# Two VectorE instructions change places at the end of each output tile

## The chip, the cores and the metric

The kernel runs on one core of a Trainium2 chip (trn2). The metric is the device time of one execution in microseconds (us), as the median of several runs. One further execution was taken with the hardware profiler; all profile lines come from it.

## The reference

Two stages follow each other, for B = 4 batches of N = 12,480 tokens with C = 128 channels, and 49 agents per batch.

```python
def sm(a, b):
    s = scale * (a @ b.transpose(0, 2, 1))
    e = np.exp(s - s.max(-1, keepdims=True))
    return e / (e.sum(-1, keepdims=True) + 1e-09)
agent_v = sm(agents, k) @ v          # 49 x 128 for each batch
x = sm(q, agents) @ agent_v          # 49,920 tokens x 128
r = np.maximum(x @ w_in, 0.0)        # 2,048 hidden channels
out = (r * r) @ w_out                # 49,920 x 128
```

The kernel folds `agent_v @ w_in` into one weight `W` of 49 rows for each batch, so that the hidden channels come straight from the 49 probabilities of a token.

## The kernel before

**Precision.** The large products are made with pairs: a value is rounded to the matmul's format (`hi`, here `gh`), the remainder is a second value (`lo`, here `gl`), and TensorE adds three products: hi by hi, hi by lo, lo by hi.

**The main loop.** The 49,920 tokens fall into 104 output tiles of `TT` = 480 tokens. A tile has 8 steps (`NJ`), and each step handles 256 of the 2,048 hidden channels, 832 steps in all. Step `i` has these parts:

- `mm1(i)`, TensorE (L364): six matmuls give the hidden values `h`, two banks of PSUM; there are two such buffers.
- `relu(i)`, ScalarE (L370): reads `h` and writes half of a buffer `rg` for two steps, which are called a pair.
- After the odd step of a pair: `square`, ScalarE (L373), in place on the whole pair, 1,920 values per partition; `high`, VectorE (L377), rounds it to `gh`; `low`, VectorE (L381), writes the remainder `gl = rg - gh`. `rg`, `gh` and `gl` have three buffers each.
- `mm2(i - 5)`, TensorE (L392): twelve matmuls of the step that lies `LAG` = 5 back, eight that read `gh` and then four that read `gl`. They add into the tile's two output banks, because the 128 contraction rows are worked in two halves at the same time, one bank for each half.

**The tile end.** After the eighth `mm2` of a tile, `store` puts the two banks together: ScalarE copies the first bank to `ob` (L397), VectorE adds the second bank (L398), and a DMA on SyncE's queue writes `ob` out (L399).

**Who wants the banks next.** There are two pairs of output banks, `pair0` and `pair1`; the tiles take them in turn. While one collects a tile, the other serves the side work of later tokens and batches: q scores and k scores (L167), transposes of the q probabilities (L338), the sums over v (L226) and the weight `W` (L277). The first side work of a tile stands on TensorE behind two further steps after the tile end, and it writes the banks that `store` has just read. Side work on the other engines includes `v_lo` (L218), `v_sum` (L242), `q_shift` (L299, L304) and `k_pmax` (L177) on VectorE, some casts on ScalarE (L214, L342), and subtractions and products on GpSimd (POOL). It is densest in three stretches of the run, in which a next batch's k and v are worked off.

**The order.** Every part is put on a list with a time, `at(t, f, ...)`, counted in steps; the list is sorted by time, and each engine gets its instructions in that order. The times are an order only: at run time each engine goes through its queue and waits where an input is missing. The set `ends` holds the steps at which a tile's last `mm2` stands (i - 5 = 7, 15, ...); each is an even step, so a pair's square, `high` and `low` come from the odd step just ahead of it. At the ends no side work is planned on ScalarE and VectorE.

Of the kernel before, what the change touches and what calls it, by code (L numbers as in the profile page):

```python
# [25 lines left out]
def agent_attention_relu2_kernel(ctx: ExitStack, tc: tile.TileContext, qT, kT, v, agT, w_in, w_out, outT):  # L26
# [379 lines left out]
    def at(t, f, *args):  # L406
        steps.append((t, len(steps), f, args))
# [5 lines left out]
    ends = {i for i in range(NG + LAG) if i >= LAG and (i - LAG) % NJ == NJ - 1}  # L413
# [172 lines left out]
    for i in range(NG + LAG):  # L586
        if i < NG:
            at(i, mm1, i)
            at(i + .1, relu, i)
            if i % 2:  # L590
                at(i + .55, square, i // 2)
                at(i + .6, high, i // 2)
                at(i + .65, low, i // 2)
        if i >= LAG:
            at(i + .2, mm2, i - LAG)
            if i in ends:
                at(i + .2, store, (i - LAG) // NJ)
# [28 lines left out]
```

## Time and profile before

| | us |
|---|---|
| median of 3 runs | 2093.01 |
| lowest and highest | 2086.31, 2101.51 |
| the profiled execution's own time | 2085.59 |
| its span, from the first to the last instruction | 2083.8 |
| TensorE (PE) busy | 2006.3 |
| weight loads (PEld) busy, beside the matmuls | 1844.0 |
| VectorE (DVE) busy | 1766.4 |
| ScalarE (ACT) busy | 1729.2 |
| GpSimd (POOL) busy | 301.2 |

The mean granted clock of TensorE is 0.984 of full speed. The DMA queues move 62 GB/s on average. In the profile's rows a name such as `ob<-ob,pair` gives the tile written and the tiles read; L398 is line 398 of the kernel. An arrow in brackets says how long the engine idled before an instruction and who ended that idle time.

### The profile page before, as it was taken

To read this page: it belongs to the slowest core of one execution; us is meant where nothing else is said; L and a number is where in the kernel's file an instruction comes from. 1 tells how busy PE (TensorE), PEld (TensorE's weight loads), DVE (VectorE), ACT (ScalarE), POOL (GpSimd) and SP (SyncE) were. 2 spreads that over 40 slices of the span, in tenths; PEclk is the share of its full clock that TensorE was granted. 3 is DMA by queue.
4 is the path that set the end of the run, shared out by engine and by line. 5 is a ranking of instruction groups with operands and counts; after the bars stand their busy time and mean duration, and the time that the engine had idled before them with its cause. 6 is when DMAs were issued, how large, how long until landed. Compare 5 with 4: busy or idle time off the path is not lost.

```text
span 2083.8 us, 45903 instructions
## 1 busy us (share of the span) xinstructions
PE 2006.3 (96%) x20130; PEld 1844.0 (88%) x20130; DVE 1766.4 (85%) x1513; ACT 1729.2 (83%) x1818; POOL 301.2 (14%) x199
## 2 busy tenths in 40 slices
PE   9899999999999999999999999999999999999999
PEld 8699988898899988988978988888887999999998
DVE  7688889899878889989887888987997888888888
ACT  2587888898878888988878788888888888888887
POOL 0100012321000102321100001232210111111010
PEclk9999999999999999999999999999999999999999
DMA  9422122121122122122112212222211111111110
GB/s 288 105 77 80 43 72 71 51 73 51 42 82 80 46 68 61 46 77 62 37 55 68 80 51 65 60 61 64 61 32 44 32 49 32 49 32 48 33 40 20
DMA packets 52849, 129.56 MB, mean 62 GB/s; under 512 B 5760, under 2 KB 21248, under 8 KB 52648
## 3 DMA queue, kind: packets, MB, share of 16 engines
q1 hardware_dynamic: 52648, 126.62, 21.3%
q8 instruction: 158, 2.59, 0.5%
q14 instruction: 43, 0.35, 0.1%
HBM read 81.47 MB, written 25.56 MB: 51 GB/s over the span
## 4 chain that ended last, share of the span: by engine, by line
PE 52%; ACT 19%; DVE 15%; issue 12%; POOL 1%; DMA 1%; SPq 0%; DVEq 0%; POOLq 0%; ACTq 0%
PE pair L392 23%; PE h L364 15%; ACT rg L373 10%; PE pair L167 8%; DVE gh L377 7%; ACT rg L370 7%; DVE gl L381 3%; PE pair L338 2%; DVE ob L398 2%; PE pair L226 1%; DVE vs L218 1%; POOL e L323 1%; PE h L167 1%; DMA vt<-v 1%; PE pair L277 1%
## 5 line engine op out<-in xcount | busy, mean ns | idle before, releaser
L370 ACT ACTIVATE rg<-h 128x960 f32<-128x960 f32 x832 | 804.2, 972 | 279.0 <-PE h L364 277.4
L381 DVE TENSOR_TENSOR gl<-rg,gh 128x1920 fp32r<-128x1920 f32 x416 | 921.2, 2214 | 30.2 <-DVE gh L377 1.8
L373 ACT ACTIVATE rg<-rg 128x1920 f32<-128x1920 f32 x416 | 756.1, 1817 | 6.1
L377 DVE CAST gh<-rg 128x1920 fp32r<-128x1920 f32 x416 | 509.7, 1225 | 230.1 <-ACT rg L373 223.8
L392 PE MATMUL pair<-gh,wo_hi 64*128 64x480 f32 x3328 | 676.9, 380 | 3.2 <-DVE acc L240 2.5
L392 PE MATMUL pair<-gh,wo_lo 64*128 64x480 f32 x3328 | 677.9, 381 | 0.0
L364 PE MATMUL h<-p_b,w_hi 49*128 49x480 f32 x1664 | 650.8, 391 | 0.0
L364 PE MATMUL h<-p_a,w_hi 49*128 49x480 f32 x1664 | 649.4, 392 | 0.3
L392 PE MATMUL pair<-gl,wo_hi 64*128 64x480 f32 x3328 | 520.5, 378 | 0.3 <-DVE gl L381 0.3
L392 PEld LDWEIGHTS pair<-gh,wo_lo 64*128 64x128 f32 x3328 | 358.8, 188 | 22.5
L392 PEld LDWEIGHTS pair<-gh,wo_hi 64*128 64x128 f32 x3328 | 355.8, 187 | 25.7 <-DVE acc L240 3.3
L392 PEld LDWEIGHTS pair<-gl,wo_hi 64*128 64x128 f32 x3328 | 351.2, 186 | 20.2 <-DVE gl L381 0.7
L364 PEld LDWEIGHTS h<-p_a,w_hi 49*128 49x128 f32 x1664 | 311.4, 187 | 16.8 <-issue 6.4
L364 PEld LDWEIGHTS h<-p_b,w_hi 49*128 49x128 f32 x1664 | 311.6, 187 | 11.1
L364 PE MATMUL h<-p_a,w_lo 49*128 49x480 f32 x832 | 316.5, 380 | 0.0
L364 PE MATMUL h<-p_b,w_lo 49*128 49x480 f32 x832 | 316.4, 380 | 0.0
L323 POOL TENSOR_TENSOR e<-e,sm 120x392 f32<-120x392 f32 x52 | 55.4, 1065 | 1278.8 <-DVE sm L320 800.4
L364 PEld LDWEIGHTS h<-p_a,w_lo 49*128 49x128 f32 x832 | 158.1, 190 | 5.6
L364 PEld LDWEIGHTS h<-p_b,w_lo 49*128 49x128 f32 x832 | 158.1, 190 | 1.5
L206 POOL TENSOR_TENSOR pe<-sk,pe 120x392 fp32r<-120x392 f32 x39 | 77.1, 1976 | 304.4 <-ACT pe L203 257.7
L330 POOL TENSOR_TENSOR pp<-e,pp 120x392 fp32r<-120x392 f32 x52 | 101.9, 1959 | 91.2 <-ACT pp L327 91.0
L167 PEld LDWEIGHTS pair<-ag_sb,qt 64*120 64x120 f32 x1600 | 88.4, 182 | 29.3 <-DVE ob L398 29.3
(93 smaller groups left out, 1341.5 us busy)
## 6 DMA issues: line engine op xcount, KB each, us to landing
vt<-v SPq DMA_DIRECT2D x104, 243.8 KB
kt<-kT SPq DMA_DIRECT2D x52, 480.0 KB
qt<-qT SPq DMA_DIRECT2D x52, 480.0 KB
outT<-ob SPq DMA_DIRECT2D x104, 240.0 KB
p_b<-p_a SPq DMA_DIRECT2D x104, 183.8 KB
raw<-w_in SPq DMA_DIRECT2D x4, 512.0 KB
raw<-w_out SPq DMA_DIRECT2D x4, 512.0 KB
ag_sb<-agT SPq DMA_DIRECT2D x1, 196.0 KB
```

The costliest lines, as they stand in the source:

```text
L167: nc.tensor.matmul(ps[:CH, u, c * A:(c + 1) * A], x[rg[u], h, c, :], ag_sb[rg[u], b, h, :], start=h == 0, stop=h == 1)
L206: eng.tensor_tensor(out=pes[n][:, :, A:], in0=piece(n), in1=pes[n][:, :, :A].bitcast(F32), op=ALU.subtract)
L323: eng.tensor_tensor(out=es[s], in0=es[s], in1=sms.pop(s).to_broadcast([CH, G, A]), op=ALU.mult)
L330: eng.tensor_tensor(out=pps[s][:, :, L:], in0=es.pop(s), in1=pps[s][:, :, :A].bitcast(F32), op=ALU.subtract)
L338: nc.tensor.matmul(pss["t", s][u][:, c, :], pp[rc[u], c, :], ident_r[rc[u], rc[u]], start=True, stop=True)
L364: nc.tensor.matmul(h[:, u, :TT], w[ra[u], j, :], PT[s][u ^ lo][ra[u], cs, :], start=x == 0, stop=x == 2)
L370: nc.scalar.activation(rgs[p][:, x], hs.pop(i)[:, :, :TT], AF.Relu)
L373: nc.scalar.activation(rgs[p], rgs[p], AF.Square)
L377: nc.vector.tensor_copy(ghs[p], rgs[p])
L381: nc.vector.tensor_tensor(out=gls[p], in0=rgs.pop(p), in1=ghs[p].bitcast(F32), op=ALU.subtract)
L392: nc.tensor.matmul(outs[t][u][:, :TT], w[rg[u], 2 * j + e, :], g[rg[u], e, :], start=j == 0 and x == 0, stop=j == NJ - 1 and x == 5)
L398: nc.vector.tensor_tensor(ob, ob, o[1][:, :TT], op=ALU.add)
```

## The change

`low` of the pair that ends just ahead of a tile end gets the time i + 1.25 instead of i + 0.65. The tile end's `store` stands at i + 1.2 in the same count, so `low` falls behind it. All other pairs stay as they were.

```diff
             if i % 2:
                 at(i + .55, square, i // 2)
                 at(i + .6, high, i // 2)
-                at(i + .65, low, i // 2)
+                at(i + (1.25 if i + 1 in ends else .65), low, i // 2)
         if i >= LAG:
             at(i + .2, mm2, i - LAG)
             if i in ends:
                 at(i + .2, store, (i - LAG) // NJ)
```

The order changes on VectorE alone; TensorE, ScalarE, GpSimd and SyncE keep every instruction in its place. VectorE's queue around tile 39 (counted from 0), in one of the stretches with work for the next batch, before:

```order
L377 CAST gh<-rg 128x1920
L381 TENSOR_TENSOR gl<-rg,gh 128x1920
L377 CAST gh<-rg 128x1920
L381 TENSOR_TENSOR gl<-rg,gh 128x1920
L398 TENSOR_TENSOR ob<-ob,pair_105 128x480
L218 TENSOR_TENSOR vs_82<-vt,vs_82 120x4x128
L377 CAST gh<-rg 128x1920
```

And of the change at the same place:

```order
L377 CAST gh<-rg 128x1920
L381 TENSOR_TENSOR gl<-rg,gh 128x1920
L377 CAST gh<-rg 128x1920
L398 TENSOR_TENSOR ob<-ob,pair_105 128x480
L381 TENSOR_TENSOR gl<-rg,gh 128x1920
L218 TENSOR_TENSOR vs_82<-vt,vs_82 120x4x128
L377 CAST gh<-rg 128x1920
```

The add (L398) stands between the rounding and the subtraction of the same pair; what follows stays. VectorE's queue around tile 87, in the later part of the run, where no work for a next batch is left, before:

```order
L320 RECIPROCAL sm<-sm 120x8
L377 CAST gh<-rg 128x1920
L381 TENSOR_TENSOR gl<-rg,gh 128x1920
L377 CAST gh<-rg 128x1920
L381 TENSOR_TENSOR gl<-rg,gh 128x1920
L398 TENSOR_TENSOR ob<-ob,pair_105 128x480
L377 CAST gh<-rg 128x1920
```

And of the change:

```order
L320 RECIPROCAL sm<-sm 120x8
L377 CAST gh<-rg 128x1920
L381 TENSOR_TENSOR gl<-rg,gh 128x1920
L377 CAST gh<-rg 128x1920
L398 TENSOR_TENSOR ob<-ob,pair_105 128x480
L381 TENSOR_TENSOR gl<-rg,gh 128x1920
L377 CAST gh<-rg 128x1920
```

Here too the two instructions have changed places and the next pair's rounding follows directly.

## The prediction

> **What bounds the kernel now.** I read first how busy each engine is, then who waits for whom, then two tile ends instruction by instruction, and last the granted clock by stretches. The page's first rows:
>
> ```profile
> span 2083.8 us, 45903 instructions
> PE 2006.3 (96%) x20130; PEld 1844.0 (88%) x20130; DVE 1766.4 (85%) x1513; ACT 1729.2 (83%) x1818; POOL 301.2 (14%) x199
> ```
>
> TensorE (PE) sets the time: it stands still for 2083.8 - 2006.3 = 77.5 us in all. VectorE (DVE) and ScalarE (ACT) have 317 us and 355 us to spare. The waits say what each engine stands for (total us, times, longest). ScalarE, VectorE, TensorE and its weight loads:
>
> ```profile
> ACT rg L370 <- PE h L364: 277.4, 210, 4.0
> ```
>
> ```profile
> DVE gh L377 <- ACT rg L373: 223.8, 208, 2.7
> ```
>
> ```profile
> PE pair L338 <- DVE ob L398: 44.3, 50, 2.9
> PE pair L167 <- DVE ob L398: 11.3, 15, 1.4
> ```
>
> ```profile
> PEld pair L167 <- DVE ob L398: 29.3, 49, 1.8
> ```
>
> ScalarE waits 210 times for TensorE's `h`, VectorE 208 times for ScalarE's square: both catch up with TensorE again and again. TensorE's own large wait is for `ob`, the add that frees the output banks: 44.3 us in front of the transposes (L338) and 11.3 us in front of the q scores (L167), 55.6 us together. The 29.3 us on the weight loads of L167 are not added: weight loads run ahead of the matmuls, and 44.3 + 29.3 + 11.3 = 84.9 us would be more than the 77.5 us that TensorE idles.
>
> **Why the add is late: two tile ends.** Tile 39, in a stretch with work for the next batch. Of VectorE, ScalarE and TensorE, each with start and length in us:
>
> ```profile
> 879.54 1.93 DVE L377 CAST gh<-rg 128x1920 fp32r<-128x1920 f32 x1 [0.91 <-ACT rg L373]
> 881.58 2.73 DVE L381 TENSOR_TENSOR gl<-rg,gh 128x1920 fp32r<-128x1920 f32 x1
> 884.23 0.64 DVE L398 TENSOR_TENSOR ob<-ob,pair 128x480 f32<-128x480 f32 x1
> ```
>
> ScalarE's copy, and the transposes on TensorE:
>
> ```profile
> 880.24 0.58 ACT L397 COPY ob<-pair 128x480 f32<-128x480 f32 x1
> ```
>
> ```profile
> 885.02 0.97 PE L338 MATMUL pair<-ident_r,pp 64*113 64x64 f32 x16 [1.75 <-DVE ob L398]
> ```
>
> And tile 87, without such work:
>
> ```profile
> 1807.98 1.62 DVE L377 CAST gh<-rg 128x1920 fp32r<-128x1920 f32 x1 [0.28 <-ACT rg L373]
> 1809.70 2.16 DVE L381 TENSOR_TENSOR gl<-rg,gh 128x1920 fp32r<-128x1920 f32 x1
> 1811.78 0.65 DVE L398 TENSOR_TENSOR ob<-ob,pair 128x480 f32<-128x480 f32 x1
> 1812.34 1.15 DVE L377 CAST gh<-rg 128x1920 fp32r<-128x1920 f32 x1
> ```
>
> ```profile
> 1808.70 0.55 ACT L397 COPY ob<-pair 128x480 f32<-128x480 f32 x1
> ```
>
> ```profile
> 1812.57 0.98 PE L338 MATMUL pair<-ident_r,pp 64*113 64x64 f32 x16 [0.75 <-DVE ob L398]
> ...
> 1814.10 0.41 PE L392 MATMUL pair<-gh,wo_hi 64*128 64x480 f32 x2
> 1814.32 0.41 PE L392 MATMUL pair<-gh,wo_lo 64*128 64x480 f32 x2
> ```
>
> In both, ScalarE's copy, which the add needs, is done (880.82 and 1809.25) before VectorE ends `gh` (881.47 and 1809.60). The add waits for nothing but its place in the row: `gl` stands in front of it, until 884.23 and 1811.78. TensorE was ready at 885.02 - 1.75 = 883.27 and at 1812.57 - 0.75 = 1811.82.
>
> **The change part by part.** Nothing is added or removed; at each tile end but the last the add and the subtraction change places.
>
> *The wait for the add.* The add starts where `gl` started: 881.58 instead of 884.23 (2.65 us earlier) and 1809.70 instead of 1811.78 (2.08 us). It ends at 882.22 and 1810.35, before TensorE comes at 883.27 and 1811.82, so both waits go. The mean wait is 44.3 / 50 = 0.89 us and 11.3 / 15 = 0.75 us; only two are longer than the 2.1 us:
>
> ```profile
> 292.65 1.70 PE L338 MATMUL pair<-ident_r,pp 64*113 64x64 f32 x15 [2.86 <-DVE ob L398]
> ```
>
> ```profile
> 373.58 0.65 PE L338 MATMUL pair<-ident_r,pp 64*113 64x64 f32 x9 [2.50 <-DVE ob L398]
> ```
>
> They leave 0.8 us and 0.4 us. With as much again for tile ends at which VectorE comes later than now, I count 53 of the 55.6 us.
>
> *The new wait in front of the add.* VectorE must now stand until ScalarE's copy is done, with `gl` queued behind. That cannot gain anything; at the two tile ends it costs nothing, since the copy was done 0.65 us and 0.35 us before the end of `gh`. Where the copy ends together with `gh` it is some tenths of VectorE's spare time, which is 317 us. Term: 0; the other end is the slow rival below.
>
> *The subtraction comes later,* by the add's step in the row: 1812.34 - 1811.78 = 0.56 us. Its reader is the last third of a `mm2` behind the transposes. In tile 87 TensorE takes 1814.10 - 1812.57 = 1.53 us from the start of the transposes over `mm1` to that `mm2`, whose four groups of `gh` matmuls follow each other by 1814.32 - 1814.10 = 0.22 us, 0.88 us in all. Starting the transposes at 1811.82 it wants `gl` at 1814.23. It ends at 1809.70 + 0.56 + 2.16 = 1812.42, 1.8 us in time. In tile 39, with the same steps from 883.27, it is wanted at 885.68 and ends at 881.58 + 0.56 + 2.73 = 884.87, 0.8 us in time. So `gl` is what comes late next; its weight loads wait for it once today:
>
> ```profile
> PEld pair L392 <- DVE gl L381: 0.7, 1, 0.7
> ```
>
> *The store* is issued 2 us earlier on SyncE's queue, its order there unchanged; nobody waits for it. Term: 0.
>
> *The clock.* Stretches of the run: PE, PEld, DVE, ACT, POOL busy us (instructions), then granted clock, DMA share, GB/s:
>
> ```profile
> 95.00:260.00 165.00, 163.49 (x1774) 152.51 (x1771) 133.02 (x108) 134.31 (x137) 11.48 (x8) 1.00 0.22 64
> 260.00:540.00 280.00, 265.75 (x2640) 247.52 (x2642) 251.77 (x213) 244.60 (x267) 63.76 (x40) 0.98 0.23 63
> 540.00:740.00 200.00, 196.26 (x2057) 178.43 (x2056) 161.09 (x136) 161.27 (x170) 14.23 (x10) 0.99 0.22 64
> 740.00:1060.00 320.00, 305.97 (x2990) 284.18 (x2988) 280.35 (x238) 276.55 (x298) 69.33 (x42) 0.97 0.21 58
> 1060.00:1260.00 200.00, 196.12 (x2068) 176.07 (x2066) 162.25 (x136) 162.32 (x170) 14.27 (x10) 1.00 0.23 65
> 1260.00:1580.00 320.00, 305.62 (x2980) 280.18 (x2978) 282.08 (x239) 276.27 (x298) 68.56 (x42) 0.97 0.20 56
> 1580.00:2080.00 500.00, 488.33 (x4710) 456.27 (x4706) 428.02 (x328) 440.93 (x427) 49.13 (x26) 1.00 0.13 37
> ```
>
> The clock was cut where TensorE idles most. The loss at full clock is 0.02 x 280 + 0.01 x 200 + 0.03 x 320 + 0.03 x 320 = 26.8 us. Close up, around tile 39, around tile 87, and at a wait of another kind (the same columns):
>
> ```profile
> 883.20:886.60 3.40, 1.65 (x26) 1.59 (x26) 3.37 (x5) 2.07 (x3) 0.00 (x0) 1.00 0.31 81
> 886.60:890.00 3.40, 3.40 (x20) 3.30 (x18) 2.74 (x2) 3.19 (x4) 0.00 (x0) 0.50 0.52 142
> 890.00:893.40 3.40, 3.40 (x40) 3.31 (x40) 2.87 (x2) 1.47 (x3) 0.00 (x0) 1.00 0.72 186
> 1811.60:1815.00 3.40, 2.65 (x34) 2.46 (x33) 3.37 (x4) 1.89 (x3) 0.00 (x0) 1.00 0.20 72
> 579.40:582.80 3.40, 2.45 (x40) 2.15 (x38) 3.24 (x5) 2.22 (x2) 0.00 (x0) 1.00 0.14 55
> 582.80:586.20 3.40, 3.40 (x20) 2.84 (x20) 2.09 (x2) 2.65 (x3) 0.00 (x0) 0.50 0.00 0
> ```
>
> After 3.4 us in which TensorE was busy for 1.65 us, the next 3.4 us ran at 0.50: 20 matmuls instead of the 40 that followed, so 1.7 us lost. After 2.65 us busy the clock stayed. The cut follows the wait, and mostly the add's. The cut at 582.80 stands behind a wait for another subtraction:
>
> ```profile
> 580.63 1.88 PE L167 MATMUL pair<-ag_sb,kt 64*120 64x49 f32 x32 [0.95 <-DVE w_lo L285]
> ```
>
> Two such cuts may stay, some 3 us. The bounds of this term are 0 and 26.8 us; I take 24, as the rows tie the cuts to the waits that go.
>
> The Trainium skill speaks against this term: "TensorE: Matmul & The Clock Gate", section "HAM oscillation — how this bites in real kernels", gives as its rule that PE-idle gaps should stay under about 3.4 us. By that rule no wait here, 2.9 us at most, touches the clock, and the sum is 24 us smaller. The row of 0.50 behind a 1.75 us wait disagrees; I go by the row and keep the rule's case as a rival.
>
> *What is given back.* In the three busy stretches TensorE idles 14.3 + 14.0 + 14.4 = 42.7 us and loses 24.8 us of clock; if all went, their 920 us became 852.5 us, with VectorE busy for 251.8 + 280.4 + 282.1 = 814.2 us, 95.5%. A pause of TensorE is also when VectorE catches up; without it some of the lateness is carried to the next tile, where `gl` has only 0.8 us of slack. Bounds: 0, and 25 us (VectorE's 814.2 us at 92% take 885 us, against some 860). I take 5, near the lower end, since VectorE still idles 106 us in these stretches today.
>
> *Sum.* The profiled execution took 2085.6 us (span 2083.8): 2085.6 - 53 - 24 + 5 = 2013.6, say **2014 us**. That execution lies 7.4 us under the median of the three runs, 2093.0, whose spread of 15 us would fit some nine clock cuts more or less; if the cuts go, the changed kernel's runs lie closer together.
>
> **The rivals.**
> *The clock stays cut.* The free transposes and scores, which keep TensorE only lightly loaded, would be enough to cut it. For: the rule above. Against: tile 87. 2014 + 24 = 2038 us.
> *VectorE becomes the bound* in the three busy stretches, by the 25 us instead of 5: 2034 us. For: 95.5%. Against: its 106 us idle there.
> *Nothing moves:* each wait taken off turns up at the next wait (`gl`, `h`), because ScalarE and VectorE pace the kernel. 2086 us. Against: they wait for TensorE 210 times.
> *Slower: the add blocks `gl`.* If ScalarE's copy ends later than `gh`, VectorE stands in front of the add and `gl` slips with it. It decides from a stand of 0.8 us (tile 39) to 1.8 us (tile 87), the slack of `gl`. At 2.2 us, one `gl` length, TensorE would wait 1.4 us and 0.4 us there, 0.9 us on average: 103 x 0.9 = 93 us, less the 55.6 us of today's waits, with the clock cuts as now: 2085.6 + 93 - 55.6 = 2123 us. For: ScalarE has a relu in front of the copy. Against: the copy ended first at both tile ends.
>
> **How the numbers follow.** Forecast 0.62, clock stays 0.13, VectorE bound 0.13, nothing moves 0.06, slower 0.06. The range goes from the sum without anything given back and with the whole clock, 2085.6 - 55.6 - 26.8 = 2003, to the clock rival with 3 us for the higher runs, 2041; it leaves out 0.12. Differences within 1% (about 21 us) are what a measurement here cannot tell from no change. Faster by over 1%: 0.62 + 0.13 + 0.13 = 0.88; within: 0.06; slower: 0.06.
>
> **What would show it.** Right: the rows "PE pair <- DVE ob" fall from 55.6 to a few us; the add starts about 0.1 us behind `gh`; the clock in the three stretches reads 0.99 to 1.00; `gl` appears as releaser of L392 with a few us at most. Wrong: a large "DVE ob <- ACT ob" (the slow rival), a large "PE <- DVE gl" (VectorE bound), or cuts to 0.50 as often as now without a wait in front (the clock rival). What would upset the forecast most is ScalarE: if it falls behind TensorE, its copy is late, and the add with it.

## The result, and the profile after

The changed kernel takes 2000.07 us (median of four runs, 1994.79 to 2001.98) against 2089.66 us before (four runs, 2083.58 to 2101.51): a ratio of 0.9561, 95% interval 0.9512 to 0.9610. Faster, as forecast, but by more: 2000 lies below the range of 2003 to 2041. The two profiled executions took 2085.6 and 1994.8 us; their 90.8 us are what the rest of the text accounts for (the forecast had 72).

The page of the changed kernel, its first rows:

```profile
span 1993.0 us, 45859 instructions
PE 1963.5 (99%) x20130; PEld 1852.2 (93%) x20130; DVE 1762.7 (88%) x1513; ACT 1725.0 (87%) x1818; POOL 308.2 (15%) x199
```

TensorE now idles 29.5 us instead of 77.5. VectorE's and ScalarE's work is the same as before to within 5 us. The waits of TensorE (total us, times, longest) show what went and what came:

```profile
PE pair L226 <- DVE e L304: 8.8, 13, 1.3
PE pair L392 <- DVE acc L240: 5.1, 3, 2.5
PE pair L167 <- DVE w_lo L285: 3.1, 4, 1.0
...
PE pair L338 <- DVE ob L398: 0.6, 1, 0.6
```

The wait for the add, 55.6 us before, is down to 0.6 us. Nearly new is a wait of the sums over v (L226) for the q subtraction (L304), 8.8 us where before had 0.8; the wait of `mm2` for `acc` grew from 2.5 to 5.1 us.

Tile 87 as VectorE, ScalarE and TensorE now run it (start, length, in us):

```profile
1724.88 1.63 DVE L377 CAST gh<-rg 128x1920 fp32r<-128x1920 f32 x1 [0.28 <-ACT rg L373]
1726.43 0.64 DVE L398 TENSOR_TENSOR ob<-ob,pair 128x480 f32<-128x480 f32 x1
1727.00 2.15 DVE L381 TENSOR_TENSOR gl<-rg,gh 128x1920 fp32r<-128x1920 f32 x1
```

```profile
1725.60 0.56 ACT L397 COPY ob<-pair 128x480 f32<-128x480 f32 x1
```

```profile
1728.09 0.64 PE L392 MATMUL pair<-gl,wo_hi 64*128 64x480 f32 x4
1728.53 0.93 PE L338 MATMUL pair<-ident_r,pp 56*113 56x56 f32 x16
1729.25 0.46 PE L364 MATMUL h<-p_b,w_hi 49*128 49x480 f32 x1
```

(The 16 transposes are of two shapes in turn; a merged row names that of one.) The add starts where the rounding ends, since ScalarE's copy ended at 1726.16. It is done at 1727.07, and the transposes start at 1728.53 with no idle time. The clock, in the three busy stretches (PE, PEld, DVE, ACT, POOL busy, then clock, DMA share, GB/s):

```profile
260.00:540.00 280.00, 274.58 (x2779) 258.41 (x2777) 264.08 (x227) 254.92 (x283) 67.90 (x42) 1.00 0.22 61
740.00:1060.00 320.00, 313.66 (x3158) 293.45 (x3157) 294.48 (x252) 289.91 (x319) 70.17 (x42) 0.99 0.23 65
1260.00:1580.00 320.00, 315.02 (x3142) 292.30 (x3141) 295.44 (x252) 291.90 (x316) 66.51 (x40) 0.99 0.20 55
```

It reads 1.00, 0.99, 0.99 instead of 0.98, 0.97, 0.97. The mean over the span rose from 0.984 to 0.996, which is 33.3 us lost before and 8.0 us now.

### The profile page after: what moved, and what is told of

It is laid out like the page before. It is cut to its first block, busy times and chain, and to the rows that moved or that the text cites. A ratio compares the mean times of both kernels' runs of the same rounds, so it can differ in the third digit from the quotient of the medians.

```text
span 1993.0 us, 45859 instructions
## 1 busy us (share of the span) xinstructions
PE 1963.5 (99%) x20130; PEld 1852.2 (93%) x20130; DVE 1762.7 (88%) x1513; ACT 1725.0 (87%) x1818; POOL 308.2 (15%) x199
## 4 chain that ended last, share of the span: by engine, by line
PE 74%; DVE 10%; ACT 10%; issue 5%; DMA 0%; DVEq 0%; SPq 0%; ACTq 0%
PE pair L392 40%; PE h L364 22%; PE pair L167 7%; ACT rg L373 4%; ACT rg L370 4%; DVE gl L381 3%; DVE gh L377 3%; PE pair L338 2%; DVE vs L218 1%; PE pair L226 1%; PE h L167 1%; PE pair L277 1%; PE pair L494 1%; DMA vt<-v 0%; DVE e L304 0%
## 5 line engine op out<-in xcount | busy, mean ns | idle before, releaser
L381 DVE TENSOR_TENSOR gl<-rg,gh 128x1920 fp32r<-128x1920 f32 x416 | 916.1, 2202 | 19.0 <-DVE gh L377 0.5
L377 DVE CAST gh<-rg 128x1920 fp32r<-128x1920 f32 x416 | 518.2, 1246 | 149.8 <-ACT rg L373 144.2
L364 PE MATMUL h<-p_b,w_hi 49*128 49x480 f32 x1664 | 643.4, 387 | 0.0
L364 PE MATMUL h<-p_a,w_hi 49*128 49x480 f32 x1664 | 640.6, 387 | 0.2
L392 PEld LDWEIGHTS pair<-gh,wo_hi 64*128 64x128 f32 x3328 | 362.5, 184 | 23.1 <-DVE acc L240 6.4
L392 PEld LDWEIGHTS pair<-gh,wo_lo 64*128 64x128 f32 x3328 | 365.4, 186 | 16.5
L364 PEld LDWEIGHTS h<-p_a,w_hi 49*128 49x128 f32 x1664 | 306.9, 185 | 16.1 <-issue 6.9
L323 POOL TENSOR_TENSOR e<-e,sm 120x392 f32<-120x392 f32 x52 | 54.5, 1048 | 1225.6 <-DVE sm L320 1132.3
L167 PEld LDWEIGHTS pair<-ag_sb,qt 64*120 64x120 f32 x1600 | 94.2, 181 | 1.2
```

Source lines behind the costliest of these rows:

```text
L167: nc.tensor.matmul(ps[:CH, u, c * A:(c + 1) * A], x[rg[u], h, c, :], ag_sb[rg[u], b, h, :], start=h == 0, stop=h == 1)
L323: eng.tensor_tensor(out=es[s], in0=es[s], in1=sms.pop(s).to_broadcast([CH, G, A]), op=ALU.mult)
L364: nc.tensor.matmul(h[:, u, :TT], w[ra[u], j, :], PT[s][u ^ lo][ra[u], cs, :], start=x == 0, stop=x == 2)
L377: nc.vector.tensor_copy(ghs[p], rgs[p])
L381: nc.vector.tensor_tensor(out=gls[p], in0=rgs.pop(p), in1=ghs[p].bitcast(F32), op=ALU.subtract)
L392: nc.tensor.matmul(outs[t][u][:, :TT], w[rg[u], 2 * j + e, :], g[rg[u], e, :], start=j == 0 and x == 0, stop=j == NJ - 1 and x == 5)
```

## Where the 90.8 us come from

| term | forecast, us | measured, us |
|---|---|---|
| shown idle time in front of side work, for the add | -53 | -55.0 |
| halved clock | -24 | -25.3 |
| given back: waits for `e` (+8.0) and `acc` (+2.6), less 3.6 of all other idle time | +5 | +7.0 |
| no term in the forecast (what is left over) | 0 | -17.5 |
| all | -72 | -90.8 |

The first and the third line together are the fall of TensorE's idle time, 77.5 - 29.5 = 48.0 us. The clock's last digit is worth some 2 us (0.001 x 2000), so the last line is good to a few us only. The three terms came out within some 2 us each. What was missing is a fourth. Theory A: a wait of TensorE costs more than the idle time shown in front of its matmuls. Rival B: the shown idle time is all, and the rest has another cause, for example the subtraction's place on VectorE. For the clock, rival C: the cuts do not hang on these waits.

## The experiments

**The change in the busy stretches alone, and in all others alone.** In these, `busy` is the list of tiles 9 to 19, 34 to 45 and 60 to 71. Every ratio from here on is to before, run again on the same chip.

```diff
-                at(i + .65, low, i // 2)
+                at(i + (1.25 if i + 1 in ends and (i + 1 - LAG) // NJ in busy else .65), low, i // 2)
```

> The add goes in front of the subtraction only at tiles 9 to 19, 34 to 45 and 60 to 71, the three busy stretches; the other tile ends stay as before. There before shows 34 us of idle time in front of 35 tile ends, and nearly all of the halved clock. Theory A (a wait costs more than the idle time that the profile shows, because the next group of matmuls also loses its overlap with the group ahead, some 0.25 us a wait; and the clock cuts hang on these waits): 34 + 9 + 24 - 8 given back = 59 us less than before. Rival B (a wait costs the idle time that is shown; the rest of the gain has another cause): about 50 us less. Rival C (the cuts have nothing to do with these waits): 35 to 43 us less and a mean clock of 0.984 as before. The waits for the add that are left: about 21 us.

Ratio to before 0.9769 (0.9739 to 0.9800), some 48 us less: what B gave, and 11 us short of A's 59. The profiled execution's span is 2029.0 us, 54.8 us less, with a mean clock of 0.997. The shown waits for the add fell by 32.8 us, and the new waits for `e` and `acc` cost 10.3 us, about as in the changed kernel; TensorE's idle time as a whole fell by 77.5 - (2029.0 - 1975.7) = 24.2 us, and the halved clock costs 27.2 us less: 51.4 us. C is out: the cuts went with the waits of these 35 tile ends. By its ratio this run sides with B; in the profiled execution 3.4 us are left over, where A put 9.

> The reverse: the add goes in front of the subtraction at all tile ends but those of the three busy stretches. Before shows 21 us of idle time there, and no clock cut behind it. Theory A: 21 + some 30 waits x 0.25 = 29 us less, with the clock cuts of the busy stretches as often as before (mean clock 0.98 to 0.985). Rival B: 21 us less. In the last stretch, where every second tile end shows 0.75 us of idle time and the clock is full, two tiles took 34.96 us: A gives 33.97 us, B 34.2 us.

Ratio 0.9817 (0.9795 to 0.9838), some 38 us less. The profiled execution's span is 2040.8 us, 43.0 us less. Both are more than either theory gave. The clock is 0.985, as in before (2.7 us). The waits of the matmuls, and below them those of the weight loads, in this kernel:

```profile
PE pair L338 <- DVE ob L398: 23.8, 18, 2.8
PE pair L167 <- DVE ob L398: 10.9, 12, 1.4
```

```profile
PEld pair L338 <- issue: 30.5, 18, 3.2
PEld pair L167 <- DVE ob L398: 18.4, 17, 1.8
```

And the weight loads of before, the row of the transposes, which the prediction did not use (its second row, 29.3 us, it did):

```profile
PEld pair L338 <- issue: 63.1, 50, 3.2
```

On the matmuls only 55.6 - 34.7 = 20.9 us of idle time for the add went, and 77.5 - (2040.8 - 1988.7) = 25.4 us of all idle time. With the 2.7 us of clock, 14.9 of the 43.0 us stand in no idle row of the matmuls (10 to 13 us of the 38 that the ratio gives); A put some 8 us there, B nothing. B is wrong. On the weight loads 92.4 - 48.9 = 43.5 us of idle time went. That this is so near the gain is chance: in the changed kernel the same rows fell by some 91 us, where the add's waits were worth 55.0 + 17.5 = 72.5 at most. How the hidden part comes about can be read in the last stretch, where the clock is full. In before:

```profile
1811.22 0.60 PE L392 MATMUL pair<-gl,wo_hi 64*128 64x480 f32 x4
1812.57 0.98 PE L338 MATMUL pair<-ident_r,pp 64*113 64x64 f32 x16 [0.75 <-DVE ob L398]
1813.36 0.46 PE L364 MATMUL h<-p_a,w_hi 49*128 49x480 f32 x1
```

The last `gl` matmuls started at 1811.22, the transposes at 1812.57, 1.35 us later; in the changed kernel 1728.53 - 1728.09 = 0.44 us. That is 0.91 us less, of which the idle column showed 0.75: the next group starts 0.44 us after the start of a `gl` group that is shown as 0.60 to 0.64 us long, and idle time is counted only from that modelled end. The transposes themselves, up to the next `mm1`, went from 0.79 to 0.72 us. And the q scores, every second tile, show no idle time of the matmuls in before, only of the weight loads:

```profile
1829.13 1.76 PEld L167 LDWEIGHTS pair<-ag_sb,qt 64*120 64x120 f32 x32 [0.23 <-DVE ob L398]
```

```profile
1829.13 1.88 PE L167 MATMUL pair<-ag_sb,qt 64*120 64x49 f32 x32
1830.83 0.46 PE L364 MATMUL h<-p_a,w_hi 49*128 49x480 f32 x1
```

The same in the changed kernel, weight loads and matmuls:

```profile
1744.79 1.88 PEld L167 LDWEIGHTS pair<-ag_sb,qt 64*120 64x120 f32 x32
```

```profile
1745.00 1.79 PE L167 MATMUL pair<-ag_sb,qt 64*120 64x49 f32 x32
1746.60 0.46 PE L364 MATMUL h<-p_b,w_hi 49*128 49x480 f32 x1
```

Where the loads run 0.21 us ahead, the group takes 1.60 us; where they wait and start with the matmuls, 1.70. Together 0.91 + 0.07 + 0.10 = 1.08 us for two tiles; two tiles went from 34.99 us (transposes at 1812.57 and 1847.56) to 33.86 us (1728.53 and 1762.39).

**Only where no idle time is shown.** The sharpest test of that: the change at 28 tile ends (the list `quiet`; tiles 50 and 76 are not in it) at which before shows no idle time of the matmuls.

```diff
-                at(i + .65, low, i // 2)
+                at(i + (1.25 if i + 1 in ends and (i + 1 - LAG) // NJ in quiet else .65), low, i // 2)
```

> The add goes in front of the subtraction only at the 28 tile ends at which before shows no idle time of TensorE at all in front of the side work (tiles 2, 4, 6, 8, 20 to 32, 48 to 58 and 74 to 98, even ones). If the idle time shown is all that a wait costs, nothing changes: two tiles of the last stretch still take 34.97 us. If a wait of the weight loads alone costs too (0.23 us idle of the weight loads in front of the q scores, which then take 1.70 instead of 1.60 us): 34.87 us for two tiles, and about 3 us less in all, which the times alone cannot tell.

Two neighbouring transposes of the last stretch:

```profile
1805.48 0.98 PE L338 MATMUL pair<-ident_r,pp 64*113 64x64 f32 x16 [0.71 <-DVE ob L398]
```

```profile
1840.33 0.98 PE L338 MATMUL pair<-ident_r,pp 64*113 64x64 f32 x16 [0.73 <-DVE ob L398]
```

They stand 34.85 us apart, with the shown waits still there, and the ratio is 0.9970 (0.9946 to 0.9995). A gave 34.87 us. The eleven such distances of the last stretch read 34.83 to 34.88 us here and 34.96 to 35.11 us in before, so the difference is clear: a wait that no matmul row shows cost some 0.1 us.

**Side work one step later, VectorE's order as before.** Another way to take the wait away.

```diff
-                at(g + .5, f, *args)
+                at(g + (1.3 if e == "PE" and (g - LAG) % NJ == 1 else .5), f, *args)
```

> VectorE's order stays as before (subtraction in front of the add). Instead TensorE takes the first side work of each tile (scores, transposes, sums over v) one step later, behind the next mm1 and mm2, some 2 us. If what costs is TensorE's wait for the banks, the wait goes here too: 1995 to 2015 us, clock 0.99 or more, waits for the add under 5 us, some of the gain lost to readers of the side work that now come later. If the place of the subtraction on VectorE does something else that is worth time: no more than half of the gain, 2040 us or more.

2004.75 us, ratio 0.9616 (0.9592 to 0.9640), clock 0.998, and no wait for the add among TensorE's matmuls:

```profile
span 1997.4 us, 45966 instructions
PE 1960.5 (98%) x20130; PEld 1829.1 (92%) x20130; DVE 1767.9 (89%) x1513; ACT 1726.9 (86%) x1818; POOL 311.5 (16%) x199
```

In its place the sums over v wait more:

```profile
PE pair L226 <- DVE e L304: 14.6, 15, 1.6
```

Four profiled executions, each against the single one of before (2083.8 us, 77.5 us idle, clock 0.984), in us and good to a few us:

| | span less | TensorE's idle time less | halved clock less | left over |
|---|---|---|---|---|
| the change | 90.8 | 48.0 | 25.3 | 17.5 |
| busy stretches alone | 54.8 | 24.2 | 27.2 | 3.4 |
| all other tile ends alone | 43.0 | 25.4 | 2.7 | 14.9 |
| side work later | 86.4 | 40.6 | 29.3 | 16.5 |

With VectorE's order untouched the fourth term is there all the same. So the gain, with its fourth term, hangs on TensorE's wait and not on the place of the subtraction on VectorE.

**The add even later.** `store` is split; the copy stays, the add and the store go to `at(i + 1.62, add, ...)`, behind the next pair's rounding (the add is L402 there).

```diff
+    def add(t):
+        ob, o = obs.pop(t)
         nc.vector.tensor_tensor(ob, ob, o[1][:, :TT], op=ALU.add)
...
                 at(i + .2, store, (i - LAG) // NJ)
+                at(i + 1.62, add, (i - LAG) // NJ)
```

> The opposite of the change: the add goes even further back, behind the rounding of the next pair. In the last stretch of before that pair's rounding takes 1.15 us, so every wait of TensorE for the add grows by some 1.2 us: about 50 waits of 2 us in front of the transposes and about 50 of 0.6 to 1.2 us in front of the q scores, 140 to 160 us of shown idle time instead of 55.6. If the clock is cut behind 3.4 us in which TensorE was busy for about 2 us or less, cuts come in the last stretch too, where before has none, and the mean clock falls to 0.95 to 0.97: 2210 to 2250 us. If only idle gaps above 3.4 us cut the clock, it stays at 0.98, the last stretch stays at 1.00, and the time is 2170 to 2195 us.

2407.52 us, ratio 1.1549 (1.1511 to 1.1587): the direction was right, the size far off. The waits grew more than forecast. A likely reason, not tested alone, is that each pause of TensorE also delays the square for which the rounding, and now the add, must wait:

```profile
PE pair L338 <- DVE ob L402: 110.5, 50, 3.4
PE pair L167 <- ACT rg L370: 54.4, 31, 2.3
```

With the other rows in front of the scores it is about 209 us. And the clock: 0.909 on average, which is at most 0.091 x 2398.0 = 218 us (its rise and that of the idle time come to some 334 us, more than the 314 us by which the execution is longer, so the two overlap). The last stretch, at 1.00 in before, and two neighbouring windows in it, with the wait in the first:

```profile
1820.00:2390.00 570.00, 525.09 (x4676) 492.09 (x4674) 422.17 (x325) 443.77 (x426) 38.15 (x26) 0.92 0.11 32
```

```profile
2087.20:2090.60 3.40, 1.55 (x24) 1.18 (x22) 3.13 (x4) 1.38 (x2) 0.00 (x0) 1.00 0.07 24
2090.60:2094.00 3.40, 3.40 (x20) 3.31 (x20) 0.96 (x1) 2.13 (x4) 0.00 (x0) 0.51 0.14 48
```

```profile
2089.64 0.97 PE L338 MATMUL pair<-ident_r,pp 64*113 64x64 f32 x16 [1.85 <-DVE ob L402]
```

TensorE busy for 1.55 us of 3.4 us, then 3.4 us at half clock. The rule of the Trainium skill ("TensorE: Matmul & The Clock Gate", section "HAM oscillation — how this bites in real kernels"), that gaps should stay under about 3.4 us, does not protect a kernel like this one: here the cut follows a wait of 1.85 us.

**What is left: order or load?** These start from the changed kernel, with the changed kernel beside them on the same chip.

> The changed kernel once more, beside the next one on the same chip: 1995 to 2002 us, 8.8 us of waits of the sums over v for the q subtraction, mean clock 0.994 to 0.996.

2000.66 us, ratio 0.9611 (0.9577 to 0.9644).

```diff
-                at(g + .5, f, *args)
+                at(g + (1.3 if f is v_acc and (g - LAG) % NJ == 3 else .5), f, *args)
```

> The changed kernel, with the sums over v (L226) one step later on TensorE wherever they stand second in a tile, behind the next mm1 and mm2. Their wait for the q subtraction (13 times, 8.8 us of shown idle time) should go as the wait for the add went in the run with the later side work: 9 us plus some 0.2 us a wait, 10 to 13 us less than the changed kernel, 1983 to 1991 us. Rival: VectorE is at 94 to 95% in the busy stretches and simply comes late at the next place (acc, gl or the third side work): no more than 4 us less.

1999.40 us against 2000.66: the same. The wait for `e` is gone from its list, and TensorE's weight loads stand for `gl` (6.6 us, 20 times) and for ScalarE's relu (7.5 us, 13 times) instead. The rival was right. To see whether VectorE's load is behind it, the next one leaves out v's remainder (zeros are put in its place once, at the start):

```diff
-        eng.tensor_tensor(out=vs[:, :, C + 2:], in0=vts[n][:, halves[h], :C], in1=vs[:, :, :C].bitcast(F32), op=ALU.subtract)
+        return
```

> The changed kernel beside the next three on the same chip: 1995 to 2002 us.

> Changed kernel, with the remainder of v left out (78 VectorE instructions of 0.78 us, 61 us, nearly all in the three busy stretches; zeros stand in its place, so the output loses that part). If VectorE, 92% busy in these stretches after the change, holds what TensorE still waits there (8.8 us for the q subtraction and 5.1 us for acc): both go, 12 to 18 us less, 1980 to 1988 us. If those waits come from the order alone, they stay and the time falls by 4 us at most.

1981.55 us against 1999.40 for the changed kernel beside it, 17.9 us less, and of the wait for the q subtraction this is left (that for `acc` L240 is gone):

```profile
PE pair L226 <- DVE e L304: 1.1, 3, 0.4
```

So in the busy stretches VectorE, 93% busy (264.08 + 294.48 + 295.44 = 854 of 920 us), does hold TensorE, for some 18 us. The remainder of v moved to GpSimd instead (`eng=nc.gpsimd` in `v_lo`):

> Changed kernel, with the remainder of v on GpSimd instead of VectorE. GpSimd takes 2.0 us for 120x392, so about 2.6 us for 120x512, 78 times: 200 us more on GpSimd, 61 us less on VectorE. But VectorE's rounding took 1.93 us instead of 1.15 us, and its subtraction 2.73 instead of 2.16 us, where GpSimd worked beside it; at a quarter more over 200 us that is 50 us back on VectorE. Expected: no gain, 1995 to 2010 us. Rival: the slowing has another cause, then as without the remainder, 1980 to 1988 us.

2033.85 us, 34 us slower than the changed kernel. VectorE's two large groups in this kernel, then in the changed one:

```profile
L381 DVE TENSOR_TENSOR gl<-rg,gh 128x1920 fp32r<-128x1920 f32 x416 | 952.2, 2289 | 20.1 <-DVE gh L377 1.4 <-PE h L364 0.5
L377 DVE CAST gh<-rg 128x1920 fp32r<-128x1920 f32 x416 | 545.1, 1310 | 176.0 <-ACT rg L373 170.5 <-PE pair L392 0.5
```

```profile
L381 DVE TENSOR_TENSOR gl<-rg,gh 128x1920 fp32r<-128x1920 f32 x416 | 916.1, 2202 | 19.0 <-DVE gh L377 0.5
L377 DVE CAST gh<-rg 128x1920 fp32r<-128x1920 f32 x416 | 518.2, 1246 | 149.8 <-ACT rg L373 144.2 <-issue 0.2
```

They cost 36.1 + 26.9 = 63 us more, as much as was taken off VectorE, and GpSimd itself became late (27.1 us of waits for `e`, 6.0 us for `pp`).

**The subtraction later still.** The subtraction behind all of the next step's VectorE parts:

```diff
-                at(i + .65, low, i // 2)
+                at(i + 1.55, low, i // 2)
```

> The subtraction goes behind every VectorE part of the next step (side work of even steps), not only behind the add. The changed kernel has a new wait of 8.8 us of the sums over v for the q subtraction (L304), which stands behind a subtraction gl. If that wait is of the same kind, it goes: 5 to 12 us less than the changed kernel, 1983 to 1995 us. Rival: gl, which has 0.8 us of slack in the busy stretches, becomes late by up to 1 us more, waits of mm2 for gl of 10 us or more appear, and the time is 2000 us or more.

1995.73 us, ratio 0.9574 (0.9554 to 0.9594). The wait that it was meant to remove stayed: 7.8 us instead of 8.8.

> The subtraction behind all of the next step's VectorE parts, once more, now beside the changed kernel on one chip. If the 4 us between their medians on different chips are real: 1993 to 1997 us, 3 to 6 us less than the changed kernel. If they are the chip's: the same within 2 us.

1993.42 us (1993.00 to 1996.93) against 1999.40 us (1997.11 to 2002.09): 6.0 us, 0.3%, less than the changed kernel, and the ranges do not overlap. Why is open. The subtractions took 2169 instead of 2202 ns on average, 14 us less in all, but the roundings 1272 instead of 1246 ns, 11 us more, and GpSimd's products (L323) 2517 instead of 1050 ns; that fits two engines that meet at other moments, but no run isolated it.

## Why the prediction was wrong

*Bound by TensorE, add late because of its place in the row:* right. The add starts at the end of the rounding, the wait went, and most of the gain (79 us by the medians, against 90) came when TensorE's side work was moved instead.

*The wait term, 53 us:* this is the step that failed. The idle time shown in front of the matmuls fell as forecast (55.0 us), but the prediction took it for the whole price of the waits ("I count 53 of the 55.6 us"), and put what the weight loads show at nothing ("The 29.3 us on the weight loads of L167 are not added"). That the rows cannot be added in full (84.9 us against 77.5 us idle) was correct; that nothing is left besides the idle time was not. The waits were worth some 17 us more, and the lower end of the range, 2003 us, had counted on no more than the idle time. In the last stretch a wait also cost the overlap of two groups of matmuls (0.16 us), and a group whose weight loads could not run ahead was 0.07 to 0.10 us longer; at 34 tile ends (49 waits of the weight loads, 15 of the matmuls) only this last part existed. An estimate from these rows for all waits is 50 x 0.23 + 15 x 0.26 + 34 x 0.10 = 18.8 us, against the 17.5 left over; most of it is the overlap, 65 x 0.16 = 10.4 us. Over the two halves it does not split as measured: the same reckoning gives 7.4 us for the busy stretches and 11.0 for the others, where 3.4 and 14.9 were left over. So the hidden price is shown in the last stretch; its size in the busy stretches stays open.

*The new wait in front of the add, 0:* right; VectorE's waits for ScalarE's copy went from 2.7 to 3.7 us.

*The clock, 24 us:* right (25.3). That two cuts or so stay behind waits of other kinds was right too. After the start of the run two are left, right behind these:

```profile
1045.18 1.88 PE L167 MATMUL pair<-ag_sb,kt 64*120 64x49 f32 x32 [0.95 <-DVE w_lo L285]
```

```profile
1262.70 0.77 PE L392 MATMUL pair<-gh,wo_hi 64*128 64x480 f32 x2 [2.46 <-DVE acc L240]
```

*Given back, 5 us:* 7.0 of idle time, with 10.6 of new waits in it. The place was wrong: not `gl` but the sums over v behind the q subtraction, and `acc`. The reason, VectorE's load in the busy stretches, was right; leaving 61 us of its work out made the changed kernel 17.9 us faster. No run leaves that work out of the kernel before, so how much of the 17.9 us the change itself gave back is not shown.

*The rivals:* none came about with its time. The clock rival (the clock stays cut) is refuted: in the changed kernel, in the two halves of the change, with the later side work and with the later add, the cuts went and came with the waits.

## What to carry to other kernels

An instruction that frees a buffer for the bounding engine belongs in front of a longer one whose reader is far off; the slack of the one that is put back (here 0.8 to 1.8 us) is the condition. Price a wait of TensorE from the start of one group to the start of the next: the idle time in front of its matmuls was too low a price here (55.0 us for some 72), and the weight loads' own rows too high (91 us). Price the half-clock window behind it as well. When the wait has gone, ask which engine was resting in it: here it was VectorE, whose load in the busy stretches now costs some 18 us, and moving its work to GpSimd made that worse.

## What the runs showed of the hardware

A pause of TensorE of 1.75 us in a window of 3.4 us was followed by 3.4 us at half clock; with pauses of some 2.1 us at nearly every tile (209 us in 100 waits) the mean clock fell to 0.909. Waits that the matmul rows do not show at all cost about 0.1 us each: two tiles of the last stretch took 34.96 to 35.11 us in before and 34.83 to 34.88 us where only such waits were removed. VectorE's 128x1920 instructions took 4 to 5% longer on average when GpSimd was given v's remainder, 182 us of new work.
